# A fused attention and two mixture-of-experts layers: smaller stores, a tile of its own, and moved subtractions at the seam between the mixtures

## The chip, the cores and the metric

The kernel runs on one core of a Trainium2 chip. The metric is the time of one execution on the device in microseconds (us), as the median of several runs; lower is better. A profiled execution gives the times of single instructions.

## What is computed

```python
attn = softmax(cap * tanh(q @ k.T / 8 / cap)) @ v          # 4 x 12 heads, 448 tokens, 64 wide
x = attn as 1792 tokens of 768
# first mixture: each token goes to the best of 8 experts
logits = x @ w_gate + modality_bias[modality_id]
x1[token] = gate_w[token] * (relu(x @ w1[e]) @ w2[e])      # 768 -> 1024 -> 768
# second mixture: each expert takes 224 tokens, greedily by the largest logits
flat = (x1 @ moe2_w_gate).flatten()
for idx in argsort(-flat): assign token to expert if both are free
out[mask_e] = relu(x1[mask_e] @ moe2_w1[e]) @ moe2_w2[e]
```

All arrays are float32.

## The kernel before

**Stages.** Attention comes first. The first mixture then works on four items (0 to 3) of 480 token slots each, the second mixture on eight items (4 to 11) of 224 tokens, one for each expert. Every float32 product is made of three matmuls on rounded halves: the weight's high part `wh` with the data's high and low part, and the weight's low part `wl` with the high part. A weight tile (768 KB) is loaded by SyncE, ScalarE copies it to `wh` (line 344), and VectorE subtracts to get `wl` (line 348). `w_split` does both; with its argument `later` the subtraction is put into a list `pend` and done by `flush`. Only the subtraction issues the load of the weight tile three places further on (`w_ahead`), since the raw tile's buffer is then free.

**The last product of the first mixture** (`last_product`, `last_tile`). The second layer of items 2 and 3 is made in twelve column blocks `k` of 128, in the order of the list `LAST`: item 2's columns 0 to 639, item 3's columns 0 to 639, item 2's columns 640 to 767, item 3's columns 640 to 767. Each `k` has eight blocks `f` of three matmuls, so there are 96 blocks `n = 8k + f`. Twelve blocks share a weight tile, `(2, 2, 0)` to `(2, 2, 7)`. After a `k`, `last_out` copies the result out of PSUM to `yt`, and two blocks into the next `k`, `last_rows` transposes it to token rows, scales them by the gate and writes them into the tile `yy`. `store_y` sends `yy` to the DRAM buffers `y_d` on ScalarE's queue: `y_d[0]` holds columns 0 to 639, `y_d[1]` the rest. In the version before it sends 640 columns of item 2 after block 42, 640 columns of item 3 after block 82, then item 2's last 128 and item 3's last 128.

```python
YY[2] = YY[3] = mp["r"].tile([128, 4, DM], F32, name="yy", tag="yy")
yt, c0 = YT[3][:, k % 3], 0 if (it, d) == (2, 5) else 128 * d    # last_rows: item 2's last rows over columns 0 to 127
```

**What sets the order around it.** The table `stream` says after which block ScalarE copies which weight tile. Beside the product runs the second mixture's token choice, in seven steps (`step`). A step compares on VectorE (`C`, line 1373), counts with narrow matmuls on TensorE (`pc`), makes a flag on VectorE (`fl`, line 1380), spreads it with a matmul (`pn`, line 1383), and prepares the next compares. These pieces are put between the product's matmuls by a clock of 218 ns a matmul (`tick`): `STEP_A` ns after the compares come the counting matmuls, and `STEP_W` ns more for each subtraction that `flush` put behind the compares (a "look"). `flush` is also called at every new weight tile and ahead of every entry of `stream`. After the steps, `positions` makes the token lists `idx2` with sixteen narrow matmuls (`pi`), and `settle` branches on whether the choice is done, ahead of the second mixture's gathers.

**The seam.** `gather2_rows(4, 0)` gathers item 4's rows from `y_d[0]` on GpSimd, `gather2_rows(4, 1)` from `y_d[1]`. `x_trans` transposes them (line 702), ScalarE and VectorE make the high and the low part (lines 704 and 705). `g1_halves` makes the first three quarters of item 4's first layer in two passes over the 128-row parts of the input, with six accumulators: a first pass, a last `x_trans` inside it, and a second pass; a pair of matmuls (lines 712 and 713) is one part of one accumulator, 36 pairs in all. The transposes' PSUM tiles come from one ring of two banks, for `last_rows` and `x_trans` alike. The fourth quarter follows in `g1`.

## Time and profile before

| what | value |
|---|---|
| median of 3 runs | 812.73 us (812.41 to 813.6) |
| the profiled execution | 814.61 us |
| its span | 812.7 us |
| TensorE matmul, busy | 782.6 us, 96% |
| VectorE, ScalarE, GpSimd, busy | 459.4, 406.5, 122.4 us |
| bytes moved by DMA | 133.88 MB, 165 GB/s over the span |

TensorE is busy nearly throughout, so an average says little: what counts is where it waits, and what it waits for. The last product of the first mixture runs from 439 to 528 us, and the second mixture follows to the end. In the rows below PE is TensorE's matmul, PEld its weight load, DVE VectorE, ACT ScalarE, POOL GpSimd. A row of a timeline gives start and length, line, operation, tiles, count, and in brackets the idle time ahead of it with what ended it.

### The profile page before, as it was taken

The numbers are of one execution on the slowest core, as the hardware profiler recorded it, in microseconds if no ns is written. First come the engines' busy times: TensorE is split into PE (matmuls) and PEld (weight loads), VectorE is DVE, ScalarE is ACT, GpSimd is POOL, SyncE is SP. The second block draws the span as 40 slices with busy tenths as digits, with TensorE's granted clock in tenths as the row PEclk, the third lists the DMA queues.
The fourth block names the chain that finished last, engine by engine and source line by source line (L and its number), as shares of the span: only waits on it lengthen the run. The fifth ranks groups of instructions, "written<-read, shape, count | busy, mean of one in ns | idle before, by whom it ended". The sixth has DMA issues, their size and how long they took to land. (4 is left out here: it accounts for less than half of the span.)

```text
span 812.7 us, 11854 instructions
## 1 busy us (share of the span) xinstructions
PE 782.6 (96%) x4804; PEld 611.5 (75%) x4804; DVE 459.4 (57%) x732; ACT 406.5 (50%) x469; POOL 122.4 (15%) x145
## 2 busy tenths in 40 slices
PE   7999999999999999999999999979999999999995
PEld 3445445444688888777877778769999999999995
DVE  5676878786535741533453663237657566565651
ACT  6886888677224331423332332436655555565550
POOL 3300303004130010010000100030601501321010
PEclk8899999999999999999999999979999999999998
DMA  7752352354544354674561242554966877787641
GB/s 241 233 207 72 102 180 72 107 178 114 173 137 166 116 151 117 207 231 130 150 163 42 55 119 87 166 178 136 321 210 210 273 222 224 240 243 230 201 151 34
DMA packets 97374, 133.88 MB, mean 165 GB/s; under 512 B 6428, under 2 KB 84380, under 8 KB 97308
## 3 DMA queue, kind: packets, MB, share of 16 engines
q1 hardware_dynamic: 87476, 104.69, 40.8%
q0 software_dynamic: 5728, 22.42, 8.7%
q10 hardware_dynamic: 4104, 5.90, 3.0%
q8 instruction: 40, 0.66, 0.3%
q14 instruction: 26, 0.21, 0.1%
HBM read 110.58 MB, written 22.41 MB: 164 GB/s over the span
## 5 line engine op out<-in xcount | busy, mean ns | idle before, releaser
L348 DVE TENSOR_TENSOR wl<-wr,wh 128x1536 fp32r<-128x1536 f32 x96 | 168.1, 1757 | 98.9 <-ACT wh L344 93.6
L344 ACT ACTIVATE wh<-wr 128x1536 fp32r<-128x1536 f32 x96 | 141.3, 1480 | 24.6 <-PE p L820 10.2
L712 PE MATMUL p<-xx,wh 128*128 128x448 f32 x372 | 120.2, 380 | 1.0 <-DVE hs L718 1.0
L780 PE MATMUL p<-xx,wh 128*128 128x480 f32 x384 | 117.4, 386 | 0.0
L713 PE MATMUL p<-xx,wl 128*128 128x224 f32 x372 | 99.5, 268 | 0.0
L571 ACT ACTIVATE ee<-pss 128x896 f32<-128x896 f32 x84 | 73.9, 910 | 41.3 <-PE pss L570 40.6
L904 PE MATMUL p<-wh,hh 128*112 128x384 f32 x240 | 82.3, 343 | 0.0
L904 PE MATMUL p<-wh,hl 128*112 128x384 f32 x240 | 80.9, 337 | 0.0
L904 PE MATMUL p<-wl,hh 128*112 128x384 f32 x240 | 80.8, 337 | 0.0
L780 PEld LDWEIGHTS p<-xx,wh 128*128 128x128 f32 x384 | 70.1, 188 | 13.0 <-issue 2.4
L712 PEld LDWEIGHTS p<-xx,wh 128*128 128x128 f32 x372 | 71.1, 191 | 7.2 <-DVE hs L718 1.3
L780 PE MATMUL p<-xx,wl 128*128 128x480 f32 x192 | 73.2, 381 | 0.0
L713 PEld LDWEIGHTS p<-xx,wl 128*128 128x128 f32 x372 | 72.2, 194 | 0.0
L587 PE MATMUL uu<-ee,vr 128*64 128x448 f32 x288 | 66.5, 572 | 0.0
L573 ACT ACTIVATE ee<-ee,capt 128x1792 f32<-128x1792 f32 x36 | 64.5, 1792 | 1.2
L1689 POOL DMA_INDIRECT xg<-y_d,idx x32 | 36.3, 1134 | 168.3 <-DMA wr<-in_moe_w_dram 79.2
L786 ACT ACTIVATE hh<-p 128x960 fp32r<-128x960 f32 (+1 forms) x17 | 15.7, 925 | 90.3 <-PE p L780 90.3
L787 DVE SCALAR_TENSOR_TENSOR hl<-p,hh 128x960 fp32r<-128x960 f32 (+1 forms) x17 | 18.7, 1099 | 66.9 <-ACT hh L786 66.9
L705 DVE TENSOR_TENSOR xx<-xp,xx 128x480 fp32r<-128x480 f32 (+2 forms) x49 | 30.8, 629 | 37.4 <-ACT xx L704 30.0
L704 ACT ACTIVATE xx<-xp 128x480 fp32r<-128x480 f32 (+2 forms) x49 | 26.8, 547 | 49.4 <-PE xp L702 49.4
L676 POOL TENSOR_TENSOR xo<-xo,rd 112x768 f32<-112x768 f32 x16 | 28.3, 1796 | 151.5 <-DVE xo L638 93.6
L570 PE MATMUL pss<-qh,wh 64*128 64x448 f32 (+1 forms) x168 | 41.8, 455 | 4.4 <-ACT ee L571 3.2
(344 smaller groups left out, 1342.5 us busy)
## 6 DMA issues: line engine op xcount, KB each, us to landing
wr<-in_moe_w_dram SPq DMA_DIRECT2D x88, 768.0 KB, 4.4
wr<-in_moe_w_t_dram SPq DMA_DIRECT2D x8, 768.0 KB, 6.7
wr<-in_k_dram SPq DMA_DIRECT2D x11, 512.0 KB, 5.4
vr<-in_v_dram SPq DMA_DIRECT2D x12, 448.0 KB
x_d<-xo SPq DMA_DIRECT2D x16, 336.0 KB, 3.9
wr<-in_q_dram SPq DMA_DIRECT2D x11, 448.0 KB, 3.4
y_d<-yy ACTq DMA_DIRECT2D x4, 1200.0 KB, 7.9
y_d<-zero POOLq DMA_DIRECT2D x1, 4480.0 KB
```

The lines of the kernel that those rows point to most:

```text
L344: AC.activation(hi, t, AF.Copy)
L348: VE.tensor_sub(lo, t, hi)
L570: PE.matmul(o, a[hs, p, ks], c[hs, p], start=j == 0, stop=j == 2)
L571: AC.activation(t[:, n % 2], ps[:, :, :S], AF.Tanh)
L573: AC.activation(t, t, AF.Exp, scale=capt[:, 0:1])
L587: PE.matmul(uu[m, p][64 * h:64 * h + 64], vt[:, 6 * p + 3 * h + r], weights(m, n)[:, h], start=n == 0, stop=n in (2, 6))
L705: VE.tensor_sub(xl[:, d0:d0 + dn], pt, xh[:, d0:d0 + dn])
L712: PE.matmul(acc, wh[:, d], xx[:, d].rearrange("p a t -> p (a t)"), start=d == 0, stop=False)
L713: PE.matmul(acc[:, :T], wl[:, d], xx[:, d, 0], start=False, stop=d == HP - 1)
L780: PE.matmul(ps[:, i, :T], a[:, d, fs], c[:, d], start=n == 0, stop=n == 3 * HP - 1)
L904: PE.matmul(acc[g][:pw], a[:, gs], c[:, i], start=f0 + i == 0 and n == 0, stop=f0 + i == 7 and n == 2)
L1689: GP.indirect_dma_start(out=t[:P, g, parts[n]], out_offset=None, in_=y_d[n][:4 * SL + N, :], in_offset=bass.IndirectOffsetOnAxis(ap=idx2[: ...
```

## The change

Six things change.

- `store_y` is cut: `store_cols` stores columns 0 to 255, 256 to 511 and 512 to 639 of each item, each as soon as its rows are written, so that only 128 columns of item 3 are stored where 640 were.
- Item 2's last rows go to a tile `yl` of their own.
- After the last `k`, ScalarE copies all 480 columns to `yt`; the row transposes fill two PSUM tiles of two groups each, and ScalarE reads the first, VectorE the second. Before, the two halved the copy and alternated on one PSUM tile.
- Item 3's last store stands ahead of `x_trans`; only columns 0 to 511 of item 4 are transposed ahead of the product, and 512 to 767 inside it. The first pass takes four parts and the second two (before five and one).
- The third weight tile of item 4's first layer is copied and subtracted behind those transposes, not after block 89; the first two go from blocks 75 and 81 to 77 and 82, and `settle` from 70 to 74.
- `flush` at a new weight tile runs only if that tile's own subtraction is still in the list. `STEP_A` and `STEP_W` grow.

```diff
-STEP_A, STEP_B, STEP_W = 3200, 700, 900
+STEP_A, STEP_B, STEP_W = 3300, 700, 1500
...
-            later.append((clock[0], rest))
+            later.append((clock[0], (it, kind, j), rest))
...
-        for ds in (range(5), range(5, HP)):
+        for ds in (range(4), range(4, HP)):
...
-        yt, c0 = YT[3][:, k % 3], 0 if (it, d) == (2, 5) else 128 * d
-        pt = ps_tr([128, 4, 128], "yp")
-        for g in range(4):
-            PE.transpose(pt[:GW, g], yt[:, g * GW:(g + 1) * GW], ident)
-        for g in range(4):
-            o = YY[3][:GW, g, c0:c0 + 128]
-            if k == 11 and g % 2:
-                VE.tensor_scalar(o, pt[:GW, g], gate(it)[:GW, g:g + 1], None, op0=OP.mult)
-            else:
-                AC.activation(o, pt[:GW, g], AF.Copy, scale=gate(it)[:GW, g:g + 1])
+        yt = YT[3][:, k % 3]
+        if (it, d) == (2, 5):
+            YY["last"] = mp["l"].tile([128, 4, 128], F32, name="yl", tag="hl3", bufs=1)
+            o = YY["last"]
+        else:
+            o = YY[3][:, :, 128 * d:128 * d + 128]
+        n = 2 if k == 11 else 4
+        for g0 in range(0, 4, n):
+            pt = ps_tr([128, n, 128], "yp")
+            for g in range(n):
+                PE.transpose(pt[:GW, g], yt[:, (g0 + g) * GW:(g0 + g + 1) * GW], ident)
+            for g in range(n):
+                if g0:
+                    VE.tensor_scalar(o[:GW, g0 + g], pt[:GW, g], gate(it)[:GW, g0 + g:g0 + g + 1], None, op0=OP.mult)
+                else:
+                    AC.activation(o[:GW, g], pt[:GW, g], AF.Copy, scale=gate(it)[:GW, g:g + 1])
...
-              75: (4, 1, 0), 81: (4, 1, 1), 89: (4, 1, 2)}
+              77: (4, 1, 0), 82: (4, 1, 1)}
...
-    def flush(age=0):
+    def flush(age=0, upto=None):
...
-        while pend and clock[0] - pend[0][0] >= age:
-            pend.pop(0)[1]()
+        while pend and clock[0] - pend[0][0] >= age and (upto is None or any(p[1] == upto for p in pend)):
+            pend.pop(0)[2]()
...
-                    flush()
+                    flush(0, (2, 2, n // 12))
...
-                if n == 70:
+                if n == 74:
                     settle()
-                if f == 2 and k == 5:
-                    store_y(2, 0)
-                elif f == 2 and k == 10:
-                    store_y(3, 0)
-                    gather2_rows(4, 0)
-                elif f == 2 and k == 11:
-                    store_y(2, 1, 0)
+                if f == 1 and k > 0:
+                    it, d = LAST[k - 1]
+                    if d in (1, 3):
+                        store_cols(it, 128 * d - 128, 128 * d + 128)
+                    elif d == 4:
+                        store_cols(it, 512, 640)
+                        if it == 3:
+                            gather2_rows(4, 0)
+                    elif d == 5:
+                        store_cols(2, 640, 768)
...
-        acc, o, half = P2["last"][k % 2][:, 0, :SL], YT[3][:, k % 3], SL // 2 if k == 11 else SL
-        AC.copy(o[:, :half], acc[:, :half])
-        if half < SL:
-            VE.tensor_copy(o[:, half:], acc[:, half:])
+        AC.copy(YT[3][:, k % 3], P2["last"][k % 2][:, 0, :SL])
...
-        wplan.append((4, 1, 3))
+        wplan.extend([(4, 1, 2), (4, 1, 3)])
...
+    def store_cols(it, c0, c1):
+        n = int(c0 >= parts[1].start)
+        y, o = (YY["last"], 640) if (it, n) == (2, 1) and "last" in YY else (YY[it], 0)
+        AC.dma_start(y_d[n][it * SL:(it + 1) * SL, c0 - parts[n].start:c1 - parts[n].start]
+                     .rearrange("(g p) c -> p g c", p=GW), y[:GW, :, c0 - o:c1 - o])
...
     last_rows(11)
-    x_trans(4, 2, P, ((0, 2), (2, 2), (4, 1)))
     store_y(3, 1)
+    x_trans(4, 2, P, ((0, 2), (2, 2)))
+    w_split(4, 1, 2)
     w_split(4, 1, 3)
...
-            g1_halves(4, T2, lambda: x_trans(4, 2, P, ((5, 1),)))
+            g1_halves(4, T2, lambda: x_trans(4, 2, P, ((4, 2),)))
```

ScalarE's queue at the seam, from the product's last 15 blocks to the first weight copy of the second mixture, before (`wh` is a weight copy, `yt` the copy out of PSUM, `yy` the scaled rows, `y_d` a store, `xx` the high part of the second mixture's input):

```order
L344 ACTIVATE wh<-wr 128x1536
L1209 DMA y_d_67<-yy 120x4x640
L883 COPY yt<-p_3889 128x480
L835 ACTIVATE yy<-yp,gtr 120x128 x4
L344 ACTIVATE wh<-wr 128x1536
L1209 DMA y_d_68<-yy 120x4x128
L883 COPY yt<-p_3890 128x240
L835 ACTIVATE yy<-yp,gtr 120x128 x2
L704 ACTIVATE xx<-xp 128x2x224 x2
L704 ACTIVATE xx<-xp 128x224
L1209 DMA y_d_68<-yy 120x4x128
L344 ACTIVATE wh<-wr 128x1536
```

And now, where `yl` is the new tile:

```order
L1215 DMA y_d_67<-yy 120x4x128
L344 ACTIVATE wh<-wr 128x1536
L891 COPY yt<-p_3889 128x480
L841 ACTIVATE yl<-yp,gtr 120x128 x4
L1215 DMA y_d_68<-yl 120x4x128
L891 COPY yt<-p_3890 128x480
L841 ACTIVATE yy<-yp,gtr 120x128 x2
L1215 DMA y_d_68<-yy 120x4x128
L704 ACTIVATE xx<-xp 128x2x224 x2
L344 ACTIVATE wh<-wr 128x1536 x2
```

The weight copy that stood between item 2's last rows and the last `yt` copy is now behind the `xx` copies, and the last store is ahead of them.

VectorE's queue around the subtraction of the third weight tile (`wl_5129`), before, in the second step of the token choice (`pc_5123` is that step's count):

```order
L1373 TENSOR_TENSOR C0_2093<-dw_2097,offc_103 120x256
L1373 TENSOR_TENSOR C1_2094<-dw_2097,offc_103 120x256
L348 TENSOR_TENSOR wl_5129<-wr_3704,wh_5128 128x1536
L1380 SCALAR_TENSOR_TENSOR fl_2099<-pc_5123,gain_104 32x16
L1384 TENSOR_TENSOR rj_3925<-dd_2095,pn_5124 120x128
```

And now, in the third step (`pc_5195`):

```order
L1383 TENSOR_TENSOR C0_2093<-dw_2097,offc_103 120x256
L1383 TENSOR_TENSOR C1_2094<-dw_2097,offc_103 120x256
L348 TENSOR_TENSOR wl_5129<-wr_3704,wh_5128 128x1536
L1390 SCALAR_TENSOR_TENSOR fl_2099<-pc_5195,gain_104 32x16
L1394 TENSOR_TENSOR rj_3925<-dd_2095,pn_5196 120x128
```

The same subtraction stands one step later, behind the next step's compares. The fifth weight tile's (`wl_5342`) stands in the same way behind the sixth step's compares. On TensorE 19 matmuls lie between the second step's flag matmul and the first matmul that reads `wl_5129`, and 17 between the fifth step's and the first that reads `wl_5342`.

## Rows read from the trace of the kernel before

**Rows 1.** Busy time by stretch: stretch, length, then busy us and count by engine, clock, DMA
```profile
528.20:551.90 23.70, 17.46 (x88) 15.05 (x88) 8.86 (x11) 7.96 (x14) 7.66 (x8) 0.78 0.52 155
...
551.90:780.00 228.10, 228.09 (x1405) 221.31 (x1406) 142.76 (x136) 129.24 (x150) 51.34 (x53) 1.00 0.74 230
...
531.40:541.70 10.30, 7.80 (x29) 6.36 (x29) 4.78 (x8) 3.66 (x6) 1.08 (x1) 0.50 0.49 146
...
146.00:149.10 3.10, 3.10 (x14) 1.76 (x12) 1.71 (x3) 2.04 (x3) 0.00 (x0) 0.50 0.25 54
```

**Rows 2.** TensorE's timeline at the seam
```profile
527.82 0.38 PE L820 MATMUL p<-hh,wl 128*128 128x480 f32 x1
...
530.28 0.43 PE L829 MATMUL yp<-ident,yt 128*120 128x128 f32 x2 [2.08 <-ACT yt L883]
...
532.14 0.68 PE L829 MATMUL yp<-ident,yt 128*120 128x128 f32 x2 [1.43 <-DVE yt L885]
...
536.90 0.72 PE L712 MATMUL p<-xx,wh 128*128 128x448 f32 x1
...
541.70 0.38 PE L712 MATMUL p<-xx,wh 128*128 128x448 f32 x1
...
547.07 0.36 PE L702 MATMUL xp<-ident,xg 112*128 112x112 f32 x2
...
551.91 0.48 PE L712 MATMUL p<-xx,wh 128*128 128x448 f32 x1 [0.98 <-DVE hs L718]
```

**Rows 3.** ScalarE's timeline there
```profile
519.79 0.57 ACTq L1209 DMA_DIRECT2D y_d<-yy  x1
...
522.55 0.56 ACT L883 COPY yt<-p 128x480 f32<-128x480 f32 x1 [1.42 <-PE p L820]
...
527.46 1.14 ACT L835 ACTIVATE yy<-yp,gtr 120x128 f32<-120x128 f32 x4 [4.35 <-DMA y_d<-yy]
...
528.48 1.50 ACT L344 ACTIVATE wh<-wr 128x1536 fp32r<-128x1536 f32 x1
...
537.27 0.32 ACTq L1209 DMA_DIRECT2D y_d<-yy  x1
```

**Rows 4.** VectorE's timeline there
```profile
530.01 1.76 DVE L348 TENSOR_TENSOR wl<-wr,wh 128x1536 fp32r<-128x1536 f32 x1 [7.08 <-ACT wh L344]
```

**Rows 5.** GpSimd's timeline there
```profile
528.44 0.96 POOL L1689 DMA_INDIRECT xg<-y_d,idx  x1 [79.22 <-DMA wr<-in_moe_w_dram]
...
540.62 1.10 POOL L1689 DMA_INDIRECT xg<-y_d,idx  x1 [9.98 <-DMA y_d<-yy]
```

**Rows 6.** The chain of waits there: start, us, what
```profile
529.70 4.92 DMA xg<-y_d,idx
```

**Rows 7.** Waits from 436 to 562 us: us in total, times, longest
```profile
PE yp L829 <- ACT yt L883: 2.7, 3, 2.1
...
PE pc L1379 <- DVE C L1373: 1.4, 2, 0.9
...
PE pn L1383 <- DVE fl L1380: 1.3, 1, 1.3
```

**Rows 8.** The page's costliest groups, lines 705 and 704
```profile
L705 DVE TENSOR_TENSOR xx<-xp,xx 128x480 fp32r<-128x480 f32 (+2 forms) x49 | 30.8, 629 | 37.4 <-ACT xx L704 30.0
L704 ACT ACTIVATE xx<-xp 128x480 fp32r<-128x480 f32 (+2 forms) x49 | 26.8, 547 | 49.4 <-PE xp L702 49.4
```

**Rows 9.** TensorE's timeline in the attention stage
```profile
144.19 0.65 PE L637 MATMUL px<-ident,xt 128*112 128x128 f32 x4 [1.67 <-DVE ds L625]
```

**Rows 10.** TensorE's timeline in the steps of the token choice
```profile
450.80 0.21 PE L1383 MATMUL pn<-fl,ones 32*120 32x16 f16 x1
...
454.42 0.21 PE L1376 MATMUL pn<-gain,ones 1*120 1x16 f16 x1
...
469.06 0.21 PE L1383 MATMUL pn<-fl,ones 32*120 32x16 f16 x1
```

**Rows 11.** VectorE's timeline in the steps
```profile
471.52 0.75 DVE L1373 TENSOR_TENSOR C<-dw,offc 120x256 f16<-120x256 f32 x2
```

More of the change, by code (lines that the diff above doesn't have):

```diff
@@ L1204, in gather_item, with store_y @@
         gather(it, x_d[it // 2][:, :], nf["gi"][:, g0:g0 + 4], 4, GW)
-    def store_y(it, n, c0=None):
-        c0 = parts[n].start if c0 is None else c0
-        cs = slice(c0, c0 + parts[n].stop - parts[n].start)
-        AC.dma_start(y_d[n][it * SL:(it + 1) * SL].rearrange("(g p) c -> p g c", p=GW), YY[it][:GW, :, cs])
+    def store_cols(it, c0, c1):
[3 more added lines that the diff above has]
+                     .rearrange("(g p) c -> p g c", p=GW), y[:GW, :, c0 - o:c1 - o])
+    def store_y(it, n):
+        store_cols(it, parts[n].start, parts[n].stop)
     l2 = ag.tile([128, 4, E], F32, name="l2")[:GW]
```

## Prediction

> **What bounds the kernel now.** I read the table of stages first, then the timelines of the five engines at the one stage that stands out. From 551.9 us on TensorE is busy for 228.09 of 228.10 us, so that stage can only be moved, not shortened. Between the end of the first mixture's last product and the start of the fourth weight quarter of the second mixture (528.2 to 551.9 us) TensorE is busy for 17.46 of 23.70 us, and its mean granted clock is 0.78 [rows 1]. That is the stage the change is about.
>
> TensorE's timeline shows what it waits for there [rows 2]. The last product's matmul ends at E = 527.82 + 0.38 = 528.2. The row transposes then wait 2.08 us for ScalarE's half of the copy and 1.43 us for VectorE's half. The first matmul of the second mixture starts at 536.90, which is E + 8.7. Eight pairs of matmuls then take 541.70 − 536.90 = 4.8 us (0.60 us a pair), and the next seventeen 547.07 − 541.70 = 5.37 us (0.316 us a pair). So the first eight run at half clock: from 531.4 to 541.7 the granted clock is 0.50, the 1.2 GHz level of the two [rows 1]. At 551.91 there is one more wait of 0.98 us.
>
> Why do the copies come late? ScalarE stores 640 columns of item 3 at 519.79, and its next write into the same tile (item 2's last rows, which are put over columns 0 to 127) waits for that store until 527.46. A weight copy follows at 528.48, ahead of the last copy out of PSUM [rows 3], and on VectorE the weight subtraction of 530.01 lies ahead of the other half [rows 4]. GpSimd's first gather for the second mixture reads what that store writes and starts at 528.44 [rows 5]; the row names a weight load, which happened to land last, but the program has it wait for the stores. The second gather starts at 529.70 and has landed at 534.62 [rows 6]. The store of item 3's last piece is issued at 537.27 [rows 3], behind the x transposes' copies, and GpSimd gathers from it at 540.62 [rows 5].
>
> Before E the waits of TensorE that routing causes are small: 1.4 us in two for the compares, 1.3 us in one for a flag that stands behind a subtraction, and of the 2.7 us for copies all but the 2.08 us counted above, so 0.6 us [rows 7].
>
> **The change part by part.** I count from E on both sides.
>
> *Pieces and the tile of their own.* Item 3's columns 0 to 511 now leave in two stores long before the end; only 512 to 639 (240 KB) are left at the place of the old 519.79 store, E − 8.4. The wait of ScalarE until 527.46 falls, since item 2's last rows go to another tile. When can GpSimd gather? The nearest row for 240 KB is 537.27 to 540.62, 3.35 us from issue to GpSimd's start [rows 3, 5], with little other traffic. The far end is the 1200 KB store, 519.79 to 528.44, 8.65 us. I take 4.1 us, nearer the first because of the size, with 0.75 us for the 768 KB weight load that runs beside it. The first gather then starts at E − 4.3, the second 529.70 − 528.44 = 1.26 us later, and it lands 4.92 us after that [rows 5, 6]: E + 1.9. The Trainium skill (DMA: Bandwidth & Descriptors, Anatomy of one DMA) gives 2.0 us fixed plus the bytes at 436 GB/s, which would be an estimated 2.6 us for a piece and 4.8 us for the old store; ScalarE's wait shows 7.67 us for the old store, so the trace disagrees there; with 2.6 us for the piece the product below would start 0.4 us earlier, at E + 3.6, when the banks are free.
>
> The change issues four stores more in all. Each stands on ScalarE's queue behind copies that are already done, and what is queued behind it is a weight copy or a PSUM copy that TensorE wants 1.3 us or more later. I cost them at nothing; the cover is the last product's matmuls.
>
> *The end.* ScalarE is free at E. One copy of 480 columns takes 0.56 us [rows 3], and the transposes start at E + 0.5. Two banks are filled, two transposes each (0.43 us for two, some 0.2 us for two more) [rows 2]. ScalarE empties the first and VectorE the second at the same time; four such copies took ScalarE 1.14 us [rows 3], so two take 0.6. The banks are free at E + 1.6 and E + 1.9. The x transposes need those banks and the gathers, so both are there at E + 1.9. Only two double transposes are left ahead of the product. A double transpose takes some 0.65 us, the copy 0.55, the subtraction 0.63 [rows 8]; with part of the first double transpose done before the second gather lands, the product starts at E + 4.0 instead of E + 8.7.
>
> The third weight quarter's copy and subtraction (1.50 and 1.76 us [rows 3, 4]) move behind these copies. They end by E + 7.5. The product needs them after 16 pairs, at E + 9 at the earliest. What covers them is thus 5 us of matmuls.
>
> *The first product.* All 36 pairs remain: 36 × 0.316 = 11.4 us, and 0.65 us for the double transpose inside. Item 3's last store is now issued at E + 2.0, ahead of the x copies; GpSimd gathers from E + 5.4, and the transposes ask for it after 20 pairs, at E + 10.3 or later. Before, a gather that started some 1.4 us after 540.62 was in use at 547.07 without a wait [rows 2, 5], so it needs at most 5 us, E + 11.8; I take no wait.
>
> *The clock.* I take the same loss as before, 8 × (0.60 − 0.316) = 2.3 us: TensorE still pauses three times within E to E + 4.0, for some 2 us in all. A pause of 1.67 us in the attention stage [rows 9] was followed by half clock from 146.0 to 149.1 [rows 1], while the wait of 1.3 us for the flag [rows 7] was not followed by any.
>
> *The wait at 551.91.* It was for VectorE, which was late from a weight subtraction. The second pass now has two pairs for each of its six products and so lasts 3.8 us, not 1.9. The wait falls.
>
> Sum of the stage: 4.0 + 11.4 + 0.65 + 2.3 = 18.35 us against 23.7, **5.35 us less**.
>
> *Subtractions only at looks.* All weight subtractions before the branch on the counts now stand behind a step's compares (or behind the one-hot at the end), with 1.5 us more planned for each. The waits of 1.4 and 1.3 us fall, and half of the 0.6 us. But the third and the fifth weight tile get their low part later than TensorE wants it. From a step's flag matmul to its compares VectorE needs 471.52 − 469.06 = 2.46 us [rows 10, 11], and the subtraction ends 0.7 + 1.76 us later, at 4.9; with the weight load of 0.2 the first product with it can start at 5.1. TensorE comes there after 19 and after 17 matmuls. Fifteen take 454.42 − 450.80 = 3.62 us with the flag [rows 10], so 19 take 4.5 and 17 take 4.06. The new waits are 0.6 and 1.05 us. Balance: 1.4 + 1.3 + 0.3 − 1.65 = **1.35 us less**, between 0 (if the 0.3 and half of the rest stay) and 3 (if the new waits do not show).
>
> The branch moves four blocks (of three matmuls each) later and costs what it cost. From 551.9 on nothing changes: the loads are issued by the same subtractions, ahead of their use.
>
> Total: 5.35 + 1.35 = 6.7 us. The profiled execution, 814.61 us around a span of 812.7, becomes 807.9; it stands 1.88 us above the median of the runs. From the median, 812.73 − 6.7 = **806.0 us**.
>
> **The rivals.**
>
> *A, the clock stays up.* The pauses are shorter than before and the transposes lie between them. For it: 1.3 us of waiting did no harm. Against it: 1.67 us did. All 2.3 us come back, 803.7; if the last gather then holds up the double transpose by up to 1.5 us, 805.2.
>
> *B, the last piece lands late.* It competes with a weight load, as the old store did. If GpSimd starts 8.65 us after the issue, as before, the product starts 4.55 us later than I take, 810.6; half of it, 808.3. For it: the stretch is dense with loads. Against it: a fifth of the bytes.
>
> *C, the routing stage gives nothing.* The new waits eat what the old ones give, 807.4. The branch also comes soon after the sixteen narrow matmuls that fetch the token lists; if its pause makes half clock last as long again as after the pause in attention, another 3.1 / 2 = 1.6 us are lost, 809.0.
>
> *D, slower.* The pieces queue behind each other and behind the loads, so that the last one, the only one waited for, is taken up over 4.1 + 6.7 = 10.8 us after its issue. From there on the gain is gone; at 12.5 us the time is 814.4. Against it: even the whole store was taken up after 8.65 us, and a piece has eight blocks, 24 matmuls or some 5 us, to itself before the next. The Trainium skill (DMA: Bandwidth & Descriptors, Rules for kernel authors) says to coalesce small transfers; by its 2.0 us for each, four more stores would cost 8 us, if they were on the path, and 814 would follow. No row shows a cost of that kind on the path.
>
> That the change does not do what it says (ScalarE still waiting for item 2's last rows, since their new tile lies where item 2's hidden values were) would show as B, for these are read until eight blocks before the last product's end.
>
> **How the numbers follow.** My forecast (804.5 to 807.5) 0.58, A 0.16, B 0.13, C 0.09, D 0.03, and 0.01 for no change at all. The range runs from A with the new waits absent, 803.0, to where B has lost three quarters, 809.6. A difference under 0.2% (1.6 us) cannot be told from no change in this kernel. Faster than that: 0.93; within it: 0.04, the far end of B; slower: 0.03.
>
> **What would show it.** The first gather would start some 4 us before the last product's end, not after it; ScalarE's writes of item 2's last rows would have no wait for a store; the first matmul of the second mixture would start 3.5 to 4.5 us after E; the wait before the fourth weight quarter would be gone; TensorE would wait about 0.6 and 1 us for a subtraction at the third and fifth weight tile. It would be wrong if the gather lands more than 3 us after E, or if the stage ahead of E gets longer.

## The result, and the profile after

The changed kernel takes **805.22 us** (median of 4 runs, 804.38 to 805.29); the kernel before took 812.65 us beside it (4 runs, 812.41 to 813.6). The ratio is 0.9904, 95% interval 0.9887 to 0.9921: about 1% faster, as forecast (806.0, range 803.0 to 809.6).

The profiled execution of after is one of 805.22 us with a span of 803.4 us. Busy time by stretch, first of before (the routing stage, from the product's first matmul behind a branch at 445 us, which is not the one of `settle`, to E, the end of the last product), then of after (the routing stage; the seam, to the start of the fourth weight quarter; all that follows; and two stretches at half clock). Columns as in [rows 1].

```profile
446.97:528.20 81.23, 77.47 (x458) 62.58 (x458) 38.42 (x142) 29.51 (x62) 2.18 (x1) 0.98 0.37 107
```

```profile
445.56:524.80 79.24, 77.32 (x458) 62.56 (x458) 38.40 (x142) 30.29 (x63) 4.08 (x3) 0.98 0.38 115
524.80:542.95 18.15, 15.60 (x89) 13.90 (x89) 8.36 (x10) 8.22 (x12) 6.71 (x6) 0.91 0.62 181
529.56:532.97 3.41, 3.41 (x13) 3.18 (x12) 2.76 (x3) 2.12 (x2) 2.56 (x2) 0.50 0.06 17
...
505.80:508.90 3.10, 3.10 (x11) 2.62 (x10) 1.76 (x1) 1.67 (x3) 0.00 (x0) 0.50 0.01 3
542.95:803.40 260.45, 252.11 (x1550) 244.91 (x1548) 153.29 (x147) 137.34 (x161) 54.55 (x56) 0.99 0.67 210
```

The routing stage is 1.99 us shorter, the seam 18.15 us where 23.71 were (−5.56), the rest 260.45 where 260.79 were. That is 7.9 us. The two spans differ by 9.3 us: 1.41 us of it are there at the routing stage's first matmul (445.56 for 446.97), in code that the change does not touch. About one microsecond of this comes from TensorE's clock in the attention stage, which stood at half for longer in the profiled execution of before; in the stretch below that execution got through 20 matmuls and the other through 24 (before, then after):

```profile
10.00:15.00 5.00, 5.00 (x20) 3.45 (x20) 4.11 (x5) 4.25 (x5) 0.72 (x1) 0.50 0.87 218
```

```profile
10.00:15.00 5.00, 4.02 (x24) 2.53 (x22) 4.23 (x5) 4.94 (x5) 1.30 (x2) 0.93 0.86 220
```

So below, kernels are compared by these three lengths, each counted from its own start, as well as by their times.

TensorE's timeline at the seam of after answers to [rows 2]. E is 524.42 + 0.38 = 524.80.

```profile
524.42 0.38 PE L820 MATMUL p<-hh,wl 128*128 128x480 f32 x1
525.45 0.65 PE L836 MATMUL yp<-ident,yt 128*120 128x128 f32 x4 [0.65 <-ACT yt L891]
526.60 0.41 PE L702 MATMUL xp<-ident,xg 112*128 112x112 f32 x2 [0.50 <-ACT yy L841]
527.51 0.79 PE L702 MATMUL xp<-ident,xg 112*128 112x112 f32 x6 [0.50 <-DMA xg<-y_d,idx]
529.21 0.47 PE L712 MATMUL p<-xx,wh 128*128 128x448 f32 x1 [0.91 <-DVE xx L705]
...
537.22 0.55 PE L702 MATMUL xp<-ident,xg 112*128 112x112 f32 x4
...
542.95 0.37 PE L712 MATMUL p<-xx,wh 128*128 128x448 f32 x1
```

The product starts at E + 4.41 (before E + 8.70). What it waits for there is the gather, 527.51, then the copies of the transposes. At 537.22 (the last x transposes) and at 542.95 (the fourth quarter, which waited 0.98 us before) nothing is waited for. ScalarE, for [rows 3]:

```profile
516.42 0.57 ACTq L1215 DMA_DIRECT2D y_d<-yy  x1
...
520.93 1.15 ACT L841 ACTIVATE yl<-yp,gtr 120x128 f32<-120x128 f32 x4 [1.18 <-PE yp L836]
...
524.84 0.56 ACT L891 COPY yt<-p 128x480 f32<-128x480 f32 x1 [2.77 <-PE p L820]
...
526.83 0.32 ACTq L1215 DMA_DIRECT2D y_d<-yy  x1
```

Item 2's last rows (520.93) wait for TensorE, no longer for a store; the copy of 480 columns follows E at once. GpSimd, for [rows 5], and the chain of waits, for [rows 6]:

```profile
520.99 0.96 POOL L1699 DMA_INDIRECT xg<-y_d,idx  x1 [73.18 <-PE yp L836]
522.26 0.94 POOL L1699 DMA_INDIRECT xg<-y_d,idx  x1 [0.30 <-issue]
530.05 0.94 POOL L1699 DMA_INDIRECT xg<-y_d,idx  x1 [6.85 <-DMA y_d<-yy]
531.28 1.62 POOL L1699 DMA_INDIRECT xg<-y_d,idx  x1 [0.30 <-issue]
```

```profile
522.26 5.21 DMA xg<-y_d,idx
```

The first gather starts 4.57 us after the piece's store (516.42) and 3.8 us before E; the second lands at 527.47, E + 2.7. The gather's row names TensorE's transposes, which had ended 0.1 us before; what it waits for is the store, which landed 3.6 us after its issue. In all eleven profiles with pieces the gather starts 0.97 us (within 0.01) after that landing, and 0.1 to 1.3 us after those transposes. In the routing stage TensorE now waits twice for a subtraction, at the third and the fifth weight tile; the waits for compares and for the flag [rows 7] are gone:

```profile
460.29 0.49 PE L820 MATMUL p<-hh,wl 128*128 128x480 f32 x1 [0.38 <-DVE wl L348]
...
481.82 0.48 PE L820 MATMUL p<-hh,wl 128*128 128x480 f32 x1 [0.80 <-DVE wl L348]
```

### The profile page after: what moved, and what is told of

It reads as the page before. It is cut to its first block, busy times and chain, and to the rows that moved or that the text cites. A ratio compares the mean times of both kernels' runs of the same rounds, so it can differ in the third digit from the quotient of the medians.

```text
span 803.4 us, 11855 instructions
## 1 busy us (share of the span) xinstructions
PE 777.7 (97%) x4804; PEld 609.2 (76%) x4804; DVE 458.6 (57%) x730; ACT 406.7 (51%) x468; POOL 124.9 (16%) x145
## 5 line engine op out<-in xcount | busy, mean ns | idle before, releaser
L1699 POOL DMA_INDIRECT xg<-y_d,idx x32 | 38.1, 1190 | 159.5 <-PE yp L836 73.2
L705 DVE TENSOR_TENSOR xx<-xp,xx 128x480 fp32r<-128x480 f32 (+1 forms) x48 | 30.5, 638 | 34.7 <-ACT xx L704 34.7
L704 ACT ACTIVATE xx<-xp 128x480 fp32r<-128x480 f32 (+1 forms) x48 | 26.5, 555 | 46.3 <-PE xp L702 46.3
```

Of the source, the lines that this page charges most:

```text
L705: VE.tensor_sub(xl[:, d0:d0 + dn], pt, xh[:, d0:d0 + dn])
L1699: GP.indirect_dma_start(out=t[:P, g, parts[n]], out_offset=None, in_=y_d[n][:4 * SL + N, :], in_offset=bass.IndirectOffsetOnAxis(ap=idx2[: ...
```

## The experiments

Each starts from the changed kernel. "Routing", "seam" and "rest" are the three lengths above, in one profiled execution each; the median and the ratio to the kernel before are from the timed runs. The experiments ran on other chips, on which the median of the kernel before was 813.0 to 813.8 us and its runs spread from 809.8 to 817.5; so the ratios, and the lengths, are what can be compared.

| kernel | median us | ratio (95% interval) | routing | seam | product starts | rest |
|---|---|---|---|---|---|---|
| before | 812.65 | 1 | 81.23 | 23.71 | E + 8.70 | 260.79 |
| after | 805.22 | 0.9904 (0.9887 to 0.9921) | 79.24 | 18.15 | E + 4.41 | 260.45 |
| after, again | 806.80 | 0.9924 (0.9900 to 0.9947) | 78.43 | 19.22 | E + 4.98 | 260.39 |
| one store | 808.76 | 0.9931 (0.9906 to 0.9955) | 79.21 | 21.45 | E + 7.94 | 260.40 |
| one store, old tile | 809.35 | 0.9930 (0.9906 to 0.9953) | 79.25 | 23.04 | E + 8.10 | 260.43 |
| old looks | 810.88 | 0.9964 (0.9942 to 0.9986) | 81.40 | 21.70 | E + 4.56 | 260.37 |
| old end | 807.02 | 0.9898 (0.9867 to 0.9930) | 78.34 | 19.73 | E + 5.58 | 260.44 |
| split back | 806.53 | 0.9912 (0.9884 to 0.9940) | 79.25 | 18.75 | E + 5.01 | 260.46 |
| store late | 807.61 | 0.9919 (0.9895 to 0.9942) | 79.21 | 20.21 | E + 4.84 | 260.41 |
| split back, no load | 807.27 | 0.9925 (0.9897 to 0.9953) | 78.42 | 19.42 | E + 5.38 | 260.44 |
| spread narrow matmuls | 804.38 | 0.9883 (0.9839 to 0.9927) | 76.98 | 20.04 | E + 4.56 | 260.43 |
| filling matmuls | 802.74 | 0.9863 (0.9824 to 0.9902) | 79.24 | 17.40 | E + 5.23 | 260.43 |
| all together | 803.90 | 0.9884 (0.9860 to 0.9908) | 76.66 | 19.10 | E + 5.50 | 260.42 |
| all but the split | 802.65 | 0.9864 (0.9830 to 0.9898) | 76.65 | 17.74 | E + 5.63 | 260.41 |

One relation holds in all thirteen profiles of the changed kernel and its variants: the first product starts 1.75 us after the second gather has landed where the x transposes run at full clock, and 1.97 us after it where they run at half clock (each within 0.01 us). With pieces the gather lands at E + 2.7 to 3.9, with one store at E + 6.0 and 6.1. So what delays this gather delays the product, and the copies and scalings of the last rows, which end before it lands, do not.

### The change once more

> The change once more, unaltered, beside the runs below. In three runs with other edits (old looks, late store, spread narrow matmuls) TensorE waited 1.5 to 1.9 us for the last gather, and half clock followed; two of these edits don't touch the seam. Theory (the place is on an edge: the gather of item 3's last columns starts 5.25 us after the last product's end, VectorE's two subtractions start at 5.54, and a gather that starts behind that point is issued and lands late): this kernel may show either, the fourth weight quarter starting 18.1 or some 20 us after that end, and its times spread by some 2 us. Rival (the waits come from the edits): 18.1 us again. The routing stage gives 79.2 us and the rest after the fourth quarter's start 260.4 us in either case; 805 to 807 us.

Same code, on another chip: 18.15 and 19.22 us at the seam, 79.24 and 78.43 us of routing. The theory's 20 us did not come; still, two executions of one kernel differ by 0.8 to 1.1 us in a stage, and a difference below that shows nothing. The routing stage's 0.81 us is the clock: after has six matmuls of the product at half clock behind the sixteen narrow ones, this execution none. The seam's 1.07 us begins with the store: it lands 4.6 us after its issue, not 3.6, and the first gather starts 5.56 us after it, not 4.57. The text above says that half clock followed the wait for the last gather in three runs; the traces show it behind the wait of 1.89 us alone, not behind those of 1.47 and 1.60 us.

### One store for item 3, and with the old tile

```diff
-                    if d in (1, 3):
+                    if it == 2 and d in (1, 3):
                         store_cols(it, 128 * d - 128, 128 * d + 128)
                     elif d == 4:
-                        store_cols(it, 512, 640)
+                        store_cols(it, 512 if it == 2 else 0, 640)
```

> The change, but columns 0 to 639 of item 3 leave in one store at the place of the last piece. Theory (the pieces carry the seam: the gather starts when the store before it has landed): the store takes the 8.65 us of the kernel before instead of the 4.57 us that the last piece took from its issue to the first gather, so both gathers come 4.1 us later and the product, which starts 1.74 us after the second one lands, does too: 805.2 + 4.1 = 809.3 us (808.5 to 810). Rival (the tile of its own carries the seam, the size of the store little): ScalarE still waits for nothing, so 805.2 to 806.

808.76 us, within the theory's range; but the interval of the ratio overlaps those of both series of after, so it is the profile that decides. Item 3's store and GpSimd's first gather, then TensorE:

```profile
516.16 0.57 ACTq L1215 DMA_DIRECT2D y_d<-yy  x1
...
524.86 0.96 POOL L1699 DMA_INDIRECT xg<-y_d,idx  x1 [77.27 <-PE p L820]
```

```profile
529.19 0.60 PE L702 MATMUL xp<-ident,xg 112*128 112x112 f32 x2 [3.34 <-DMA xg<-y_d,idx]
530.56 1.38 PE L702 MATMUL xp<-ident,xg 112*128 112x112 f32 x6 [0.76 <-DMA xg<-y_d,idx]
532.49 0.74 PE L712 MATMUL p<-xx,wh 128*128 128x448 f32 x1 [0.55 <-DVE xx L705]
```

The store was issued at 516.16, so the gather starts 8.70 us after it (before: 8.65), and the product at E + 7.94. That is 3.5 us later than in after (3.0 than in its second execution), of the 4.29 us that the change moved the product's start. The seam grows by 3.3 us only (2.2 against the second execution): the half clock now begins while TensorE waits and transposes (six transposes in 1.38 us, not 0.79), and some of it is over before the pairs.

```diff
-        if (it, d) == (2, 5):
-            YY["last"] = mp["l"].tile([128, 4, 128], F32, name="yl", tag="hl3", bufs=1)
-            o = YY["last"]
-        else:
-            o = YY[3][:, :, 128 * d:128 * d + 128]
+        c = 0 if (it, d) == (2, 5) else 128 * d
+        o = YY[3][:, :, c:c + 128]
```

> As the run with one store, and item 2's last rows go over columns 0 to 127 of the tile that this store reads, as before the change. Theory (the gather is what the product waits for): ScalarE waits for the store until about 0.7 us before the last product's end, its four copies and the copy out of PSUM come about 1 us late, but the second gather lands 6.7 us after that end in any case, so nothing is added to the run with one store: 809.3 us (808.5 to 810). Rival (the tile carries the seam): the run with one store is near 805.2 and this one at 809 or more.

ScalarE waits again, but is through before the gather matters:

```profile
523.77 1.14 ACT L838 ACTIVATE yy<-yp,gtr 120x128 f32<-120x128 f32 x4 [4.13 <-DMA y_d<-yy]
```

The product starts at E + 8.10, 0.16 us later than without the old tile, and the ratio is the same. The seam is 1.6 us longer because ten pairs, not five, run at half clock: it begins 4.0 us behind E in both runs, but lasts 10.2 us here and 6.8 us there. Whether the tile has a part in that is not shown. For the product's start the size of the store counts, not the tile. The old tile beside the pieces was not tried.

### The old looks

```diff
-STEP_A, STEP_B, STEP_W = 3300, 700, 1500
+STEP_A, STEP_B, STEP_W = 3200, 700, 900
...
-                    flush(0, (2, 2, n // 12))
+                    flush()
```

> The change, but the subtractions and the plan of the steps are as before the change (flushed at every weight tile, 3200 and 900 ns). Theory (the routing stage gives what its waits say): 1.35 us by the forecast, 1.99 us by the stage's length in the two profiles, so 806.6 to 807.2 us. Rival (the shorter stage is the clock or chance, the waits only move): 805.2, within 0.4.

Slower than either expected. Routing takes 81.40 us, as before the change: the looks are worth 2.2 us there (81.40 − 79.24; 3.0 us against the second execution). The rest of the loss was in nobody's expectation. At the seam the product starts as in after, but later on TensorE waits for the last gather (GpSimd, VectorE, TensorE):

```profile
532.55 2.24 POOL L1699 DMA_INDIRECT xg<-y_d,idx  x1 [6.43 <-DMA y_d<-yy]
535.09 1.36 POOL L1699 DMA_INDIRECT xg<-y_d,idx  x1 [0.31 <-issue]
```

```profile
532.22 3.43 DVE L348 TENSOR_TENSOR wl<-wr,wh 128x1536 fp32r<-128x1536 f32 x2 [0.65 <-ACT wh L344]
```

```profile
541.43 0.32 PE L702 MATMUL xp<-ident,xg 112*128 112x112 f32 x1 [1.89 <-DMA xg<-y_d,idx]
```

The gather of item 3's last columns starts at E + 6.0, not 5.25, and VectorE has begun two weight subtractions 0.3 us earlier; in after the gather (530.05) is ahead of them by as much:

```profile
530.34 3.43 DVE L348 TENSOR_TENSOR wl<-wr,wh 128x1536 fp32r<-128x1536 f32 x2 [0.65 <-ACT wh L344]
```

The issue then takes 2.24 us, where 0.93 to 0.96 is usual, its partner's starts at E + 8.6 instead of 6.5, and TensorE waits 1.89 us, with half clock behind it: eleven slow pairs in all, not six. The traces show a plain rule: an issue that starts inside a weight subtraction ends 0.80 to 0.86 us after that subtraction's end, whether it started early or late in it. This holds for 221 of the 222 such issues (of gathers and of scatters) in the fourteen profiles; the other one started 0.01 us into its subtraction and took 0.93 us. At the seam those that start outside take 0.93 to 0.96 us. So do the six that start inside a subtraction of line 705, which reads one of its inputs from PSUM (0.93 us). The Trainium skill (SBUF — State Buffer, Who interferes with whom) says that a VectorE instruction with two SBUF inputs contends with a GpSimd instruction that reads SBUF. The weight subtraction has two such inputs and the gather reads its token list there, so the rows agree. The Trainium skill also tells there of a probe in which `tensor_tensor`, the operation of these subtractions, stalled no transfer; here it holds up the issue of gathers.

### The old end

```diff
-        AC.copy(YT[3][:, k % 3], P2["last"][k % 2][:, 0, :SL])
+        acc, o, half = P2["last"][k % 2][:, 0, :SL], YT[3][:, k % 3], SL // 2 if k == 11 else SL
+        AC.copy(o[:, :half], acc[:, :half])
+        if half < SL:
+            VE.tensor_copy(o[:, half:], acc[:, half:])
...
-        n = 2 if k == 11 else 4
+        n = 4
...
-                if g0:
+                if k == 11 and g % 2:
```

> The change, but after the last block the two engines halve the copy and then take turns on one PSUM tile of four groups, as before the change. Theory (the second gather, landing 2.7 us after the last product's end, is what the product waits for): the four copies take turns and last 1.55 us instead of 0.63, but the first x transposes have the other bank; the tile is free some 2.7 to 3.1 us after that end, so 0 to 0.5 us are added: 805.2 to 805.7. Rival (one engine for each bank is worth its whole difference): 0.9 us and more, 806.1 to 806.5.

The fair partner is the second execution of after: in both the first gather starts at E − 2.8, and in both the clock holds behind the narrow matmuls. The product starts at E + 5.58 for 4.98 and the seam is 0.51 us longer, but not by the old end. The second gather's way, here and in the second execution of after (start, length):

```profile
523.65 5.20 DMA xg<-y_d,idx
```

```profile
523.73 4.57 DMA xg<-y_d,idx
```

It lands at E + 3.61 for 3.00, and the product follows 1.97 us later in both. The four scalings end at E + 2.90, not 1.95, but the gather is still not there then. So the theory's reason holds: the gather is what counts. One engine for each bank is worth nothing that shows in these executions, and the ratio is not told apart from after's.

### The third weight quarter back in the stream

```diff
-              77: (4, 1, 0), 82: (4, 1, 1)}
+              77: (4, 1, 0), 82: (4, 1, 1), 89: (4, 1, 2)}
...
-    w_split(4, 1, 2)
     w_split(4, 1, 3)
```

> The change, but the third weight quarter's copy and subtraction go back to the place after block 89. Theory (both places are covered by other work): ScalarE has 2.7 us free between item 2's last rows and the last copy out of PSUM and needs 1.5, VectorE's 1.76 us end before its two scalings: 805.2 us, within 0.5. Rival (the raw tile lands late there, so the last copy out of PSUM stands behind it, as before the change): up to the copy's 1.5 us more, 806.7.

ScalarE's last copy waits for nothing new, so the rival's reason falls; the ten runs spread from 802.7 to 811.1 us and decide nothing, and the seam's 18.75 us lie between after's two. What differs is the last store: its gather comes 6.0 us after it (3.2 and 4.1 in after's two), beside the load that the early subtraction set free. To take that load away:

```diff
             VE.tensor_sub(lo, t, hi)
-            w_ahead()
+            if (it, kind, j) != (4, 1, 2):
+                w_ahead()
```

> The third weight quarter is copied and subtracted after block 89, as in the run with the split put back, but that subtraction issues no load; the load goes out with the fourth quarter's. Theory (in that run the 768 KB load issued 0.4 us after the last product's end ran beside the second gather and the last store, and made the product start at 5.0 instead of 4.4 us and the store's gather come 6.0 us after its issue instead of 3.2): the product starts 4.4 us after the end, the store's gather 3 to 4 us after its issue, with one subtraction beside it and not two, no wait for the last gather: 805.2 us, and the fourth quarter starts 18.1 us after the end. Rival (the copy and the subtraction themselves were in the way): 5.0 us and 18.7 us, 805.8.

The edit missed its aim. The load still goes out as soon as the raw tile is free, since SyncE has nothing ahead of it; only its place in the program moved. From 2 to 5 us behind E the DMA engines are as busy as in the run before it (0.82 there; this run, then after):

```profile
527.04:530.04 3.00, 1.76 (x8) 1.24 (x8) 0.30 (x1) 0.67 (x2) 0.00 (x0) 0.62 0.90 281
```

```profile
526.80:529.80 3.00, 1.60 (x11) 1.16 (x11) 1.16 (x2) 1.84 (x3) 0.00 (x0) 0.96 0.37 89
```

So it says nothing on its theory. Whether the new place of the third weight quarter is worth anything by itself stays open: against after's two executions the seam with it put back is 0.5 us shorter to 1.3 us longer, and those two differ by 1.07.

### The last store behind the x copies

```diff
-    store_y(3, 1)
     x_trans(4, 2, P, ((0, 2), (2, 2)))
+    store_y(3, 1)
```

> The change, but item 3's last store stands behind the x transposes and their copies again. Theory (the order matters, since the old-looks run showed a gather that started 0.8 us later, met VectorE's two subtractions and kept TensorE waiting 1.89 us): the store is issued 2 us later, 4 us after the last product's end, the last gather lands after TensorE asks for it, 12.4 us after that end, by 1 to 4 us, and half clock may follow again for some 1.6 us: 806.2 to 810.8. Rival (hidden anyway, as the prediction's 5 us would have it: 4 + 3.4 + 5 = 12.4): 805.2, within 0.5.

```profile
532.20 1.62 POOL L1699 DMA_INDIRECT xg<-y_d,idx  x1 [8.36 <-DMA y_d<-yy]
534.12 1.36 POOL L1699 DMA_INDIRECT xg<-y_d,idx  x1 [0.30 <-issue]
```

```profile
539.98 0.32 PE L702 MATMUL xp<-ident,xg 112*128 112x112 f32 x1 [1.47 <-DMA xg<-y_d,idx]
```

The wait is there, 1.47 us, and the seam is 1.0 to 2.1 us longer than in after's two executions. Both issues start inside subtractions and take 1.62 and 1.36 us. Whether a gather meets a subtraction decides here, by some tenths of a microsecond.

### Narrow matmuls spread

```diff
                       start=c == 0, stop=c == NCH - 1)
+            if c % 2:
+                yield 200
```

> The change, but two of the sixteen narrow matmuls that make the token lists stand between one of the last product's matmuls and the next, not all sixteen in a row. Theory (the narrow matmuls in a row bring the half clock behind them, and what each takes is its weight load): the slow matmuls after them, six to eight at 0.18 us more than at full clock, go, 1.1 to 1.5 us, and of the 3.30 us of the row some half is hidden: 802.1 to 804.1 us. Rival (the half clock comes there whatever stands before): 804.4 to 805.4.

```profile
500.31 0.38 PE L1631 MATMUL pi<-room 120*112 120x32 f16 x2
500.54 0.47 PE L820 MATMUL p<-hh,wh 128*128 128x480 f32 x1
500.85 0.38 PE L1631 MATMUL pi<-room 120*112 120x32 f16 x2
```

```profile
444.25:521.23 76.98, 75.06 (x458) 60.89 (x458) 38.32 (x142) 30.23 (x63) 4.08 (x3) 1.00 0.40 117
```

Routing takes 76.98 us, 2.26 less than in after and 1.45 less than in its second execution, which had no slow matmul there either: no matmul behind the narrow ones is slow, and a pair delays the product by some 0.3 us where two in a row took 3.30 / 8 = 0.41. The seam gives most of it back, 20.04 us: the last gather met the subtractions again (an issue of 1.91 us at E + 6.3, a wait of 1.60 us). So the median lies between the theory's range and the rival's.

### Filling matmuls in the waits

```diff
+    P2["fill"] = ps_g([128, 512], "fill")
+    fill(3)
     last_rows(11)
+    fill(2)
     store_y(3, 1)
-    x_trans(4, 2, P, ((0, 2), (2, 2)))
+    x_trans(4, 2, P, ((0, 2), (2, 2)), (2, 4))
...
+    def fill(n):
+        w = wsplit_t[4, 1, 0][0]
+        for _ in range(n):
+            PE.matmul(P2["fill"], w[:, 0, :128], w[:, :2].rearrange("p d c -> p (d c)"), start=True, stop=True)
```

> The change, but TensorE multiplies resident weights (eleven matmuls of 512 columns in all, into a PSUM tile that nobody reads) where it waits at the seam: three after the last product, two after the row transposes, two after the first x transposes, four after the last. Theory (the waits bring the half clock that follows): the six pairs at half clock, 6 x 0.28 = 1.7 us, go, less up to 0.3 us where a filling matmul ends late: 803.5 to 803.8. Rival (the half clock follows the transposes, or comes in any case): 805.2 to 805.5.

```profile
524.51 0.89 PE L695 MATMUL fill<-wh 128*128 128x512 f32 x3
...
525.73 0.71 PE L695 MATMUL fill<-wh 128*128 128x512 f32 x2
527.24 0.38 PE L707 MATMUL xp<-ident,xg 112*128 112x112 f32 x2 [0.80 <-DMA xg<-y_d,idx]
...
528.76 1.17 PE L695 MATMUL fill<-wh 128*128 128x512 f32 x4
529.90 0.47 PE L721 MATMUL p<-xx,wh 128*128 128x448 f32 x1
```

```profile
529.90:533.30 3.40, 3.40 (x22) 3.23 (x22) 2.75 (x3) 2.47 (x2) 2.79 (x3) 1.00 0.12 34
```

802.74 us, below what either expected. No pair is slow: the clock is 1.00 where after has 0.50. The two runs with filling below have no slow pair at the seam either, and all eleven profiles without it have some. So the waits bring the half clock, and the transposes between them do not prevent it. The 36 pairs and the transposes among them take 12.2 us (17.40 − 5.23) where after needed 13.7 (18.15 − 4.41). The product starts 0.8 us later, but not behind the filling: the second gather lands at E + 3.48, not 2.66, and the product follows 1.75 us after it in both. The Trainium skill (TensorE: Matmul & The Clock Gate, What's actually happening) has the clock follow how busy TensorE has been; this run agrees, while the sixteen narrow matmuls, back to back, were followed by half clock in eight of eleven profiles all the same.

### Together

> All that looked good together: the narrow matmuls of the token lists in pairs between matmuls of the product; subtractions at a look without the wait for their age, which moves the fifth weight tile's one look forward; the third weight quarter after block 89 without its load; nine filling matmuls (three, two, one, three) at the seam. Theory (the gains add up): 2.26 us and 0.80 us in the routing stage, so some 76.2 us, and at the seam the 1.65 us of half clock less up to 0.4 us for filling matmuls that end late, so the fourth quarter starts 16.7 to 17.1 us after the last product's end: 805.2 - 4.3 = 800.9 us (800.3 to 801.5). Rival (the edge at the last gather decides): a wait of 1.5 us and half clock behind it come back, 803.5 to 804.

Routing 76.66, no slow pair, but the seam takes 19.10 us: the load of the split delays the last gather, and TensorE waits 1.15 us for it. The rival's time came.

> As the run with all together, but the third weight quarter stays at the seam, as the change has it, and ten filling matmuls (three, two, two, three). Theory (in the runs with the split put back the load that SyncE issues as soon as the raw tile is free, 0.4 us after the last product's end, cost the second gather and the last store's gather their time; without it the fourth quarter starts as in the run with filling matmuls alone, 17.4 us after the end, or 0.2 less): 76.7 + 17.2 to 17.4 + 260.4 us from the product's first matmul after the branch to the end, some 1.8 us less than the run with all together, which had 803.9 us: 802.1 us. Rival (the edge: the store's gather starts behind VectorE's first subtraction, its successor is issued late and TensorE waits 1 to 1.6 us): the fourth quarter starts at 18.5 to 19 us, 803.3 to 803.9.

```profile
446.50:523.15 76.65, 75.04 (x459) 61.23 (x460) 38.30 (x142) 30.20 (x63) 4.08 (x3) 1.00 0.39 118
523.15:540.89 17.74, 16.25 (x98) 13.69 (x98) 8.38 (x10) 8.25 (x12) 7.09 (x6) 1.00 0.66 187
```

802.65 us, between the theory's time and the rival's. With the rest of the table's row the three lengths add up to 354.80 us; after has 357.84 and 358.04. This version has the lowest median, though its ratio cannot be told from that of filling alone, and the intervals of both overlap that of after's first series. From the version before it, it differs by the place of the third weight quarter and one filling matmul, and its seam is 1.36 us shorter: the nearest that the runs come to a price for that place.

## Why the prediction was right

*The pieces.* The mechanism is the forecast's, and the run with one store shows it: with the whole store the gather starts 8.70 us after it and 3.0 to 3.5 of the 4.3 us are gone again. The size was off: I took 4.1 us from the piece's store to the gather; it was 4.57, 5.56 in the second execution, and 4.7 to 5.8 in the other runs with pieces. So the gather landed at E + 2.7 and 3.0 instead of 1.9, at the edge of what was named as a sign of being wrong (over 3 us), and past it in most of the other runs; the product started at 4.4 to 5.0, not 4.0. The 2.6 us that the prediction works out from the Trainium skill (DMA: Bandwidth & Descriptors, Anatomy of one DMA) come from a fit for transfers that GpSimd issues; these pieces, stored by ScalarE, landed 3.6 to 4.8 us after their issue. Rival B was priced 4.55 us for a whole store's delay; the whole store costs 2.2 to 3.3, since TensorE's half clock then falls partly into its wait.

*The tile of its own.* The wait of ScalarE fell as forecast, but the two runs with one store show that there it is hidden behind the gather in any case.

*The end.* One engine for each bank: banks free at E + 1.75 and 1.95 (forecast 1.6 and 1.9). The forecast has banks and gather ready at the same moment; the gather lands 0.7 us or more behind the banks, so that their gain is hidden, as the run with the old end shows.

*The clock.* Forecast 2.3 us lost, measured six pairs × (0.59 − 0.316) = 1.6 us. That the pauses are the cause was argued then and is shown now by the filling matmuls. Rival A falls: shorter pauses with transposes between them did not keep the clock up in any run; work in the pauses did.

*Item 3's last store.* "I take no wait" held for this kernel, by a step that was wrong. GpSimd's start, E + 5.25, was forecast well (5.4), and TensorE asked later (E + 12.4) than the 10.3 I took as the earliest; but the time that the gathers need was taken as fixed. Two serve these transposes, and "at most 5 us" from the second one's start is 6.4 us from the first one's. In three of the four runs that had to wait it was 7.8 to 8.9 us, since the issue of the second stands behind a first one that VectorE's subtractions hold up; in the fourth (all together) it was 5.5, but the first gather started only at E + 7.8. This is the edge that four of the experiments fell over.

*The wait at 551.91* is gone, as forecast. The sum for the seam was 18.35 us: 18.15 and 19.22 measured. That the first is so near is in part luck: the product starts 0.4 us late and the clock takes 0.7 us less.

*The looks.* Forecast 1.35 us, measured 1.99 between the profiles and 2.16 with the looks undone (2.80 and 2.97 against the second execution). The mechanism was right, down to the two new waits. They were priced 0.6 and 1.05 us and measured 0.38 and 0.80; rival C falls. In after the 0.6 us of small waits went whole, not by half. The pause at the branch of `settle` cost what it had cost, 0.30 us.

*Rival D* falls: in all runs with pieces the one that is waited for was taken up 4.6 to 5.8 us after its issue, not 10.8.

*The range.* Its ends do not follow from the terms named for them: A without the new waits is 803.7 − 1.65 = 802.1, not 803.0, and three quarters of B make 809.4, not 809.6. The result lies inside either way.

*Not tried.* No run undoes the smaller transposes ahead of the product (512 columns for 640), or the later places of the first two weight tiles and of `settle`. What they are worth by themselves is open.

## What to carry to other kernels

What the next stage waits for is the landing of the last bytes it needs: store early what is ready early, so that only a small piece is left when it counts. Count each transfer of a chain, with the issue of each, and ask which engine's instructions stand beside that issue; a margin of a few tenths of a microsecond falls either way in the next version. Where TensorE must wait in short pieces between dense stretches, idle matmuls on resident weights can be worth more than a shorter wait.

## What the runs showed of the hardware

- At the seam a gather's issue by GpSimd took 0.93 to 0.96 us. One that started inside one of VectorE's weight subtractions ended 0.80 to 0.86 us after that subtraction's end (221 of 222 in all fourteen profiles), and so took 1.10 to 2.38 us at the seam.
- A gather started 0.97 us after the landing of the piece that it waited for, in all eleven profiles with pieces.
- Sixteen narrow matmuls in a row (3.30 us, in after busy throughout at clock 1.00) were followed by up to eight of the product's at half clock in eight of eleven profiles, and by none in three, the second execution of after among them. Spread between wide ones they were not followed by any, in three profiles.
- Four waits of 0.5 to 0.9 us with transposes between them were followed by 3.4 us at half clock; with 512-column matmuls in the waits, by none, in three profiles. Single waits of 1.15 to 1.60 us in the middle of the pairs were not followed by half clock, in three runs; one of 1.89 us was.
- A store of 240 KB was taken up by GpSimd 2.9 us after its issue when little else moved, and 5.8 to 6.0 us after it beside a 768 KB load.
